# A layer kernel whose instruction order is planned again: transfers served one after another, loads set later, three-pass first tiles, warm-up in gaps

## The chip, the cores and the metric

The kernel runs on one core of a Trainium2 chip. The metric is device time in microseconds (us), the median of several executions; lower is better. The core has a matrix engine (TensorE, PE in the profile), a vector engine (VectorE, DVE), an activation engine (ScalarE, ACT), GpSimd (POOL) and a queue engine (SyncE, SP) that issues most transfers. Each engine works through its own list of instructions in order: an instruction that waits holds back all that stand behind it on that engine.

## The reference

The input x is 2048 tokens of 512 values. With xn, the layer-normed x, the output is x plus an attention part plus a part from a mixture of experts:

```
xn  = layernorm(x)
qkv = xn @ wqkv                       # 512 x 1536, 32 heads of 16
out = x + attention(qkv) @ wo         # each token sees itself and 7 tokens
                                      # at distances 2, 4, .. 14 before it
    + sum over the token's two best experts e of
        gate_e * (silu(xn @ w1[e]) @ w2[e])   # 8 experts, 512 -> 1792 -> 512
```

The two experts of a token are the largest of xn @ w_gate, and the gates are the softmax of those two logits.

## The kernel before

**Numbers.** Every float32 operand of a product is split into a high and a low float16 part (scales SW, SX, SH), and each product is three matmuls: high by high, low by high, high by low. In the QKV products these are the passes h, l and w.

**Stages on TensorE.** First the QKV products: 64 tile products, column group cg (0 to 3) by token tile j (0 to 15), named q<cg>_<j>; group 0 carries the router's logits too. A tile product is 12 matmuls (lines 348 and 350), about 2 us. They go through six PSUM banks, and ScalarE copies each result out (line 358, `ev`) into one of three buffers `qe`, from which four tiles at a time are stored to DRAM (line 367, `qst`). Then eight experts, 14 blocks each: `up` (lines 779 to 781), SiLU on ScalarE (line 787, tile hs), the split into hh (lines 793 and 797) and `down` (lines 809 to 822). At the end the product with wo (line 905).

**The token tiles' way to TensorE.** For each tile j, VectorE takes mean and variance (lines 279, 281), ScalarE the root (line 286), VectorE the normalized tile xn (lines 291, 293); `hi` (ScalarE, line 298) and `lo` (VectorE, line 302) make the float16 parts xh. TensorE needs them with the token in the free dimension (xnT): the first six tiles are turned on TensorE (line 313), the other ten by a transposing transfer `tn` of xh (line 308), issued by SP. All 16 tiles xh are also stored to DRAM (line 305, `xst`), from where the rows of each expert are gathered later. xh has six buffers: `hi` of tile j waits for both transfers of tile j-6. The QKV weights come in four groups of 768 KB (line 250, `lwq0` to `lwq3`) and are split by ScalarE and VectorE (lines 265, 262).

**The way to the experts.** After the last logits (line 363) VectorE works out the lists of rows (lines 391 to 503). GpSimd gathers the rows of an expert in up to five pieces (line 708, tile xg, five buffers), and SP issues a transposing transfer for each piece (line 715, tile xgt, `tx<e>_<t>`). Expert weights come in 57 pieces `ld<U>` of 1 MB (lines 730, 735, tile s, two buffers); ScalarE and VectorE split each (lines 745 and 754, `whi`, `wlo`). Beside this, VectorE does the attention: line 635, 639 (scores), ScalarE's exponential (line 649, `ax`), lines 662, 668 and so on, most of them 4.4 us long.

**What sets the order.** Class Plan holds every step as a task: engine, duration, dependencies, priority, and `land`, the time from a transfer's issue to its arrival. `solve` gives each task a latest time, going back from TensorE's order, and then goes forward in time: each engine takes, of the tasks that are ready, the one with the earliest latest time. `emit` writes the instructions in the order found. On the chip nothing of the planned times is left, only the order on each engine and the waits for data and buffers. The memory of xnT, the weights of QKV and `qe` is given to the expert stage by `swap_left`; the planner lets the first SiLU follow once the last `qst` has been issued, but on the chip hs takes memory that this transfer has to be done reading.

Of the kernel before, what the change touches and what calls it, by code (L numbers as in the profile page):

```python
# [44 lines left out]
WARM = 14  # L45
N32 = 6
NPE = 6
NPAIR = 8
XB = 8
NG = E * FB  # L50
# [3 lines left out]
class Plan:  # L54
    SAME = {"PE": 0.0, "DVE": 0.0, "ACT": 0.0, "SP": 0.0, "POOL": 0.0}

# [3 lines left out]
    def add(self, name, eng, dur, fn, deps=(), prio=0.0, land=0.0, early=0.0, begun=()):  # L60
        assert name not in self.tasks, name
        self.tasks[name] = (eng, dur, fn, [d for d in deps if d is not None], prio, land, early,
                            [d for d in begun if d is not None])

    def solve(self, start):
# [9 lines left out]
        for n in sorted((n for n in tk if tk[n][0] == "PE" and tk[n][4] > -900), key=lambda n: tk[n][4]):  # L75
            due[n] = at
            at += tk[n][1]
        late, todo, wait = {}, [n for n in tk if n not in outs], {n: len(o) for n, o in outs.items()}
        while todo:
            n = todo.pop()  # L80
            t = tk[n]
            l_ = due.get(n, at)
            for o in outs.get(n, ()):
                l_ = min(l_, late[o] if n in tk[o][7] and n not in tk[o][3] else late[o] - t[1] - t[5] - 0.08)
# [8 lines left out]
        begin, end, order = {}, {}, []  # L93

        def release(n):
# [11 lines left out]
        while True:  # L107
            best = None
            for e, lst in ready.items():
# [3 lines left out]
                c = min((p, r, n) for r, p, n in lst if r <= t0)  # L113
                if best is None or (t0, c[0]) < best[0]:
                    best = ((t0, c[0]), e, c)
# [6 lines left out]
            end[n] = t0 + t[1] + t[5]  # L122
# [6 lines left out]
        self.begin, self.end, self.order = begin, end, order  # L129
# [19 lines left out]
def layer_kernel(ctx: ExitStack, tc, x, wqkv, wo, wg, w1, w2, out):  # L149
# [38 lines left out]
    def c_first():  # L188
        v.memset(warm, 0.0)
        v.memset(eps, 1e-5 / (SX * SX))  # L190
# [37 lines left out]

    def warm_up(n):
        t = py.tile([P, D], F32, name="pwarm", tag="y0")  # L230
        for _ in range(n):
            nc.tensor.matmul(t, warm[:, 0:P], warm, start=True, stop=True)
# [3 lines left out]
    def load_x(g, h=None):  # L236
# [3 lines left out]
        nc.sync.dma_start(X[g][:, c_], xv[:, 2 * g:2 * g + 2, :][:, c_])  # L240
# [43 lines left out]
    def ln_rs(j):  # L284
        rs = fre.tile([P, 1], F32, name=f"rs_{j}", tag="rs", bufs=4)
        nc.scalar.activation(rs, L[j]["mv"][:, 1:2], AF.Sqrt, bias=eps, scale=1.0 / (SX * SX))
        L[j]["rs"] = rs

    def ln_nm(j):
        rs = L[j]["rs"]  # L290
        v.reciprocal(rs, rs)
# [989 lines left out]
```

## Time and profile before

| what | value |
|---|---|
| median of 3 runs | 807.27 us (805.89 to 807.44) |
| the profiled execution's own time | 804.93 us |
| its span, first to last instruction | 803.2 us |
| TensorE busy | 771.4 us, 96% of the span |
| VectorE busy | 624.8 us, 78% |
| ScalarE busy | 356.1 us, 44% |
| GpSimd busy | 115.3 us, 14% |
| mean granted TensorE clock | 0.990 of full speed |

The profile is one execution. In it, "busy" is time with an instruction running on the engine; a bracket behind a row of the timeline is the engine's idle time just before, and what ended it. SPq and ACTq rows are the issuing of transfers by SP and ACT. "PEclk" is the granted TensorE clock as a share of full speed, and the DMA share is the mean busy share of the 16 DMA engines (it can go over 1).

### The profile page before, as it was taken

To read this page: it belongs to the slowest core of one execution; us is meant where nothing else is said; L and a number is where in the kernel's file an instruction comes from. 1 tells how busy PE (TensorE), PEld (TensorE's weight loads), DVE (VectorE), ACT (ScalarE), POOL (GpSimd) and SP (SyncE) were. 2 spreads that over 40 slices of the span, in tenths; PEclk is the share of its full clock that TensorE was granted. 3 is DMA by queue.
4 is the path that set the end of the run, shared out by engine and by line. 5 is a ranking of instruction groups with operands and counts; after the bars stand their busy time and mean duration, and the time that the engine had idled before them with its cause. 6 is when DMAs were issued, how large, how long until landed. Compare 5 with 4: busy or idle time off the path is not lost.

```text
span 803.2 us, 13105 instructions
## 1 busy us (share of the span) xinstructions
PE 771.4 (96%) x5300; PEld 426.4 (53%) x5300; DVE 624.8 (78%) x591; ACT 356.1 (44%) x523; POOL 115.3 (14%) x103
## 2 busy tenths in 40 slices
PE   7978998969999999999999999999999999999996
PEld 3634665535556555555555555555555555555543
DVE  5861985999999999999999999999994333366074
ACT  4542331444445544745464465455464544544100
POOL 2000072400016001300100050010000000063061
PEclk8999999989999999999999999999999999999999
DMA  8599699943548656834894585477439833455184
GB/s 288 149 274 238 218 238 294 340 150 106 180 104 268 211 145 172 277 105 145 234 258 154 182 196 170 153 157 259 136 105 264 302 110 108 140 189 168 50 275 147
DMA packets 147075, 153.88 MB, mean 192 GB/s; under 512 B 67729, under 2 KB 115217, under 8 KB 146499
## 3 DMA queue, kind: packets, MB, share of 16 engines
q1 hardware_dynamic: 139667, 135.33, 56.2%
q0 software_dynamic: 5216, 16.88, 6.9%
q10 hardware_dynamic: 2128, 0.80, 0.4%
q8 instruction: 43, 0.70, 0.4%
q14 instruction: 21, 0.17, 0.1%
HBM read 108.12 MB, written 29.56 MB: 171 GB/s over the span
## 4 chain that ended last, share of the span: by engine, by line
PE 87%; DMA 6%; DVE 3%; ACT 1%; SPq 1%; issue 1%; ACTq 0%; POOL 0%; DVEq 0%
PE pu L779 12%; PE pu L780 12%; PE pu L781 12%; PE y L811 9%; PE y L809 9%; PE y L810 9%; PE pq L350 6%; PE pw L905 5%; PE yt L820 3%; PE yt L822 3%; PE yt L821 3%; PE pq L348 3%; DMA xnT<-xh 2%; DMA s<-in_B_w 1%; DVE at L639 1%; DMA xg<-xr,lis 1%
## 5 line engine op out<-in xcount | busy, mean ns | idle before, releaser
L779 PE MATMUL pu<-xgt,w 128*128 128x64 f16 (+8 forms) x616 | 185.2, 322 | 7.4 <-ACT hs L787 7.4
L780 PE MATMUL pu<-xgt,w 128*128 128x64 f16 (+8 forms) x616 | 185.3, 322 | 0.0
L781 PE MATMUL pu<-xgt,w 128*128 128x64 f16 (+8 forms) x616 | 181.0, 322 | 0.0
L787 ACT ACTIVATE hs<-pu 128x64 f32<-128x64 f32 (+8 forms) x154 | 69.5, 480 | 201.2 <-PE pu L781 200.4
L754 DVE SCALAR_TENSOR_TENSOR w<-s,w 128x2048 f16<-128x2048 f32 (+1 forms) x57 | 128.1, 2249 | 34.6 <-ACT w L745 34.2
L745 ACT ACTIVATE w<-s 128x2048 f16<-128x2048 f32 (+1 forms) x57 | 107.2, 1882 | 74.3 <-PE yt L822 62.1
L708 POOL DMA_INDIRECT xg<-xr,lis x35 | 72.5, 2071 | 465.1 <-DMA xgt<-xg 352.9
L811 PE MATMUL y<-w,hh 128*128 128x512 f16 x336 | 127.3, 379 | 0.0
L810 PE MATMUL y<-w,hh 128*128 128x512 f16 x336 | 127.3, 379 | 0.0
L809 PE MATMUL y<-w,hh 128*128 128x512 f16 x336 | 127.3, 379 | 0.0
L797 DVE SCALAR_TENSOR_TENSOR hh<-hs,hh 128x550 f16<-128x550 f32 (+7 forms) x112 | 76.6, 686 | 48.5 <-ACT hh L793 48.5
L350 PE MATMUL pq<-wq,xnT 128*128 128x384 f16 (+1 forms) x512 | 96.1, 331 | 15.1 <-DMA xnT<-xh 8.0
L781 PEld LDWEIGHTS <-w 128*128 128x128 f16 x616 | 59.2, 98 | 48.9 <-issue 0.8
L780 PEld LDWEIGHTS <-w 128*128 128x128 f16 x616 | 59.3, 98 | 48.7 <-issue 8.2
L779 PEld LDWEIGHTS <-w 128*128 128x128 f16 x616 | 59.6, 98 | 41.1 <-issue 0.5
L821 PE MATMUL yt<-hh,w 128*128 128x166 f16 (+7 forms) x448 | 81.0, 219 | 0.0
L820 PE MATMUL yt<-hh,w 128*128 128x166 f16 (+7 forms) x448 | 80.9, 219 | 0.0
L822 PE MATMUL yt<-hh,w 128*128 128x166 f16 (+7 forms) x448 | 80.9, 219 | 0.0
L635 DVE TENSOR_TENSOR pq<-kt,qt 128x4096 f32<-128x4096 f32 x16 | 70.7, 4421 | 7.7 <-DMA qt<-qd 7.5
L350 PEld LDWEIGHTS <-xnT 128*128 128x128 f16 x512 | 49.6, 98 | 50.6 <-DMA xnT<-xh 12.1
L793 ACT ACTIVATE hh<-hs 128x550 f16<-128x550 f32 (+7 forms) x112 | 70.6, 630 | 3.5
L662 DVE TENSOR_TENSOR pv<-vt,at 128x4096 f32<-128x4096 f32 x16 | 70.8, 4423 | 0.3
(165 smaller groups left out, 861.7 us busy)
## 6 DMA issues: line engine op xcount, KB each, us to landing
s<-in_B_w SPq DMA_DIRECT2D x112, 512.0 KB
qd<-qe SPq DMA_DIRECT2D x16, 768.0 KB
kt<-qd SPq DMA_DIRECT2D x8, 960.0 KB
vt<-qd SPq DMA_DIRECT2D x8, 960.0 KB
yd<-ys SPq DMA_DIRECT2D x24, 256.0 KB
xr<-xh SPq DMA_DIRECT2D x16, 256.0 KB
qt<-qd SPq DMA_DIRECT2D x8, 512.0 KB
acc<-in_A_x SPq DMA_DIRECT2D x4, 1024.0 KB
```

Of the source, the lines that this page charges most:

```text
L350: nc.tensor.matmul(ps[:, 0:n], xs, t[:, kb, 0:n], start=st, stop=False)
L745: nc.scalar.activation(w[:, 0, c_], stg[k][:, c_], AF.Copy, scale=SW)
L754: v.scalar_tensor_tensor(w[:, 1, c_], stg[k][:, c_], SW, w[:, 0, c_], op0=ALU.mult, op1=ALU.subtract)
L779: nc.tensor.matmul(ps, a_[:, 0, kb, fs], xh, start=kb == 0, stop=False)
L780: nc.tensor.matmul(ps, a_[:, 0, kb, fs], xl, start=False, stop=False)
L781: nc.tensor.matmul(ps, a_[:, 1, kb, fs], xh, start=False, stop=kb == KB - 1)
L809: nc.tensor.matmul(y_, hi, b_[:, 0, :], start=st, stop=False)
L810: nc.tensor.matmul(y_, hi, b_[:, 1, :], start=False, stop=False)
L811: nc.tensor.matmul(y_, lo, b_[:, 0, :], start=False, stop=sp)
L820: nc.tensor.matmul(y_, b_[:, 0, cs], hi, start=st and c % 2 == 0, stop=False, skip_group_check=True)
L821: nc.tensor.matmul(y_, b_[:, 0, cs], lo, start=False, stop=False, skip_group_check=True)
L822: nc.tensor.matmul(y_, b_[:, 1, cs], hi, start=False, stop=sp, skip_group_check=True)
```

## The change

The arithmetic stays the same in kind: the scale SX moves from the normalization into the instructions that make the float16 parts, so a copy becomes an activation with a scale, and a subtraction becomes a multiply and subtract. The order is planned with other rules, and some transfers change engine. The diff, cut to its core:

```diff
 # Plan: `land` becomes `svc`, the time a transfer occupies the one server;
 # `lead`: not ready earlier than so long before its latest time
-            end[n] = t0 + t[1] + t[5]
+            end[n] = t0 + t[1]
+            if t[5]:
+                dma = max(dma, t0 + 1.3) + t[5]
+                end[n] = dma + 0.7
...
+            if t[5]:
+                r += min(max(0.0, late[n] - r) / 4, 3.0)
+            if t[8] is not None:
+                r = max(r, late[n] - t[8])
...
+    add("root", "ACT", 1.6, lambda: nc.scalar.activation(root, eps, AF.Sqrt if not POW else AF.Copy), early=0.3)
+    for i in range(NFILL):                                    # NFILL = 6
+        add(f"warm{i}", "PE", mm(512), B(warm_up, 1), early=6.6, prio=1e6, begun=["T32_0"])
+    add("lx0", "SP", 0.45, B(load_x, 0, 0), svc=0.7, early=0.8)
-        add(f"lwq0_{kb}", "ACT", 0.62, B(load_wq, 0, [kb], nc.scalar), prio=-100 + kb, land=3.4 + 0.3 * kb, early=0.4)
-    add("lgate", "ACT", 0.62, B(load_gate, nc.scalar), prio=-90, land=3.0, deps=[], begun=["lwq0_3"])
-    add("root", "ACT", 1.5, lambda: nc.scalar.activation(root, eps, AF.Sqrt), begun=["lgate"], prio=-89)
-    add("lx1", "SP", 0.45, B(load_x, 0, 1), prio=1, land=3.0, begun=["lx0"])
+        add(f"lwq0_{kb}", "SP", 0.66, B(load_wq, 0, [kb], nc.sync), svc=0.67, begun=["lx0"])
+    add("lx1", "ACT", 0.6, B(load_x, 0, 1, nc.scalar), svc=0.7, begun=["root"])
+    add("lgate", "ACT", 0.6, B(load_gate, nc.scalar), svc=0.3, begun=["lx1"])
...
-    add("fills", "SP", 1.8, fills, deps=["lo_9"], prio=200, land=3.0)
+    add("fills", "SP", 1.2, fills, deps=["lwq1_3"], svc=1.2, early=20.0)
...
-        add(f"hi_{j}", "ACT", act(512), B(x_hi, j), deps=[f"nm_{j}", f"xst_{j - 6}" if j > 5 else None, ...
+        add(f"hi_{j}", "ACT", act(512), B(x_hi, j), early=18.0 if j < N32 else 0.0, deps=[f"nm_{j}", f"xst_{j - XH}" if j >= XH else None, ...
...                                                            # XH = 10 buffers of xh, 6 before
-            add(f"tn_{j}", "SP", 0.5, B(x_turn, j), deps=[f"lo_{j}"], prio=100 + j, land=5.5)
+            add(f"tn_{j}", "SP", 1.35, B(x_turn, j), deps=[f"lo_{j}"], svc=1.6)
...
-        if i < 4:
+        if i < NSPL:                                          # NSPL = 6
...
-                deps=["r_lis"] + prev + xst, prio=e, land=2.5)
+                deps=["r_lis"] + prev + xst, svc=0.9, lead=40.0 if e else None)
-                prio=G(e * FB - 8) if e else 20.0, land=5.5)
+                svc=1.6, lead=30.0 if e else None)
-        add(f"ld{U}", "SP", 1.4, B(piece_load, U), deps=[...], prio=G(2 * U - 6), land=6.5, ...
+        add(f"ld{U}", "SP", 1.0, B(piece_load, U), deps=[...], svc=3.0, lead=22.0, ...
```

All other transfers get an `svc` for their `land` too. The first six tile products (four before) are three tasks, h, l and w, that may stand apart, and the w passes may stand behind other tiles' passes. Six warm-up matmuls of 512 columns, on nothing but zeros, are set after the first transpose, beside the 14 at the start; they write a bank of their own. Functions that turned float16 tiles on TensorE go; no tile used them.

What this does to the order shows at three places. The first is SP's list in the QKV stage, about where the first token tiles have been normalized. xr<-xh is a store of a tile of xh, xnT<-xh a transposing transfer (the tile's number stands behind xh), wqs_2 and wqs_3 are the weights of the third and fourth column group, qd<-qe a store of results. Before:

```order
L305 DMA xr_67<-xh_2_273 128x1024
L367 DMA qd_66<-qe_0_0_236 128x6x256
L367 DMA qd_66<-qe_1_0_280 128x6x256
L250 DMA wqs_2_500<-in_A_wqkv 128x3x128 x4
L305 DMA xr_67<-xh_3_328 128x1024
L308 DMA_TRANSPOSE xnT_102<-xh_7_480 128x8x128
L305 DMA xr_67<-xh_4_331 128x1024
L305 DMA xr_67<-xh_7_480 128x1024
L250 DMA wqs_3_556<-in_A_wqkv 128x3x128 x4
L305 DMA xr_67<-xh_5_401 128x1024
L308 DMA_TRANSPOSE xnT_102<-xh_8_530 128x8x128
```

After:

```order
L253 DMA x_7_252<-in_A_x 128x1024
L263 DMA wqs_2_270<-in_A_wqkv 128x3x128 x4
L263 DMA wqs_3_320<-in_A_wqkv 128x3x128 x4
L378 DMA qd_66<-zf_85 8x16x64 x2
L379 DMA xr_67<-zf_85 512x1x128
L325 DMA_TRANSPOSE xnT_102<-xh_6_403 128x8x128
L374 DMA qd_66<-qe_0_0_247 128x6x256
L322 DMA xr_67<-xh_6_403 128x1024
L322 DMA xr_67<-xh_0_318 128x1024
L325 DMA_TRANSPOSE xnT_102<-xh_7_499 128x8x128
L374 DMA qd_66<-qe_1_0_307 128x6x256
```

The weights of the later groups and the fills now stand right behind the loads of x, ahead of the first transposing transfer; they stood between the second and third. The stores of the first tiles stand behind, among the transposing transfers.

The second place is SP's list toward the end of the QKV stage. xgt_1<-xg_1 are the transposing transfers of the second expert's five pieces, s<-in_B_w1 and in_B_w2 the halves of a piece of expert weights, kt and qt attention loads; rows named ISA, which move no data, are left out. Before:

```order
L715 DMA_TRANSPOSE xgt_1_1355<-xg_1_1_1329 128x8x128
L730 DMA s_3_1381<-in_B_w1 128x4x256
L735 DMA s_3_1381<-in_B_w2 128x2x512
L715 DMA_TRANSPOSE xgt_1_1355<-xg_1_2_1333 128x8x128
L715 DMA_TRANSPOSE xgt_1_1355<-xg_1_3_1353 128x8x128
L715 DMA_TRANSPOSE xgt_1_1355<-xg_1_4_1376 128x8x32
L367 DMA qd_66<-qe_2_3_1349 128x6x256
L367 DMA qd_66<-qe_3_0_1431 128x6x256
```

After:

```order
L374 DMA qd_66<-qe_2_3_1339 128x6x256
L737 DMA s_2_1557<-in_B_w1 128x4x256
L742 DMA s_2_1557<-in_B_w2 128x2x512
L374 DMA qd_66<-qe_3_0_1436 128x6x256
L737 DMA s_3_1608<-in_B_w1 128x4x256
L742 DMA s_3_1608<-in_B_w2 128x2x512
L374 DMA qd_66<-qe_3_1_1555 128x6x256
L374 DMA qd_66<-qe_3_2_1624 128x6x256
L737 DMA s_4_1705<-in_B_w1 128x4x256
L742 DMA s_4_1705<-in_B_w2 128x2x512
L374 DMA qd_66<-qe_3_3_1687 128x6x256
```

The second expert's transposing transfers stood ahead of the stores qe_2_3 and qe_3_0; now none of them stands ahead of the last store qe_3_3 (they come after the next pair of attention loads and s_5), and pieces of weights stand between the stores.

The third place is ScalarE's list at the end of the QKV stage: copies out of PSUM into qe_3_3 (the last four tiles), the attention's second exponential at_1, and the first SiLU, hs_0_0. Before:

```order
L358 ACTIVATE qe_3_3_1638<-pq_3_12_1607 128x3x2x64
L649 ACTIVATE at_1_1452<-at_1_1452 128x512
L358 ACTIVATE qe_3_3_1638<-pq_3_13_1625 128x3x2x64
L358 ACTIVATE qe_3_3_1638<-pq_3_14_1644 128x3x2x64
L358 ACTIVATE qe_3_3_1638<-pq_3_15_1660 128x3x2x64
L787 ACT_TABLE_LOAD
L787 ACTIVATE hs_0_0_1744<-pu_0_0_0_1675 128x486
```

After:

```order
L365 ACTIVATE qe_3_3_1687<-pq_3_12_1659 128x3x2x64
L365 ACTIVATE qe_3_3_1687<-pq_3_13_1673 128x3x2x64
L365 ACTIVATE qe_3_3_1687<-pq_3_14_1691 128x3x2x64
L365 ACTIVATE qe_3_3_1687<-pq_3_15_1708 128x3x2x64
L794 ACT_TABLE_LOAD
L794 ACTIVATE hs_0_0_1793<-pu_0_0_0_1723 128x486
```

The exponential, which stood ahead of the last three copies, now stands behind the third SiLU.

On VectorE, the small steps that work out the gates (lines 510 to 592 of the kernel before; they ran from 590 to 605 us there, with other work between) move to the time right after the first attention scores, ahead of the first split of expert weights.

More of the change, by code (lines that the diff above doesn't have):

```diff
@@ L54, with add @@
 class Plan:
-    SAME = {"PE": 0.0, "DVE": 0.0, "ACT": 0.0, "SP": 0.0, "POOL": 0.0}
     def __init__(self):
         self.tasks = {}
-    def add(self, name, eng, dur, fn, deps=(), prio=0.0, land=0.0, early=0.0, begun=()):
+    def add(self, name, eng, dur, fn, deps=(), prio=0.0, svc=0.0, early=0.0, begun=(), lead=None):
         assert name not in self.tasks, name
-        self.tasks[name] = (eng, dur, fn, [d for d in deps if d is not None], prio, land, early,
-                            [d for d in begun if d is not None])
+        self.tasks[name] = (eng, dur, fn, [d for d in deps if d is not None], prio, svc, early,
+                            [d for d in begun if d is not None], lead)
     def solve(self, start):
@@ L82, in solve @@
             l_ = due.get(n, at)
+            cost = t[1] + 0.08 + (2.5 + t[5] * 1.5 if t[5] else 0.0)
             for o in outs.get(n, ()):
-                l_ = min(l_, late[o] if n in tk[o][7] and n not in tk[o][3] else late[o] - t[1] - t[5] - 0.08)
+                l_ = min(l_, late[o] if n in tk[o][7] and n not in tk[o][3] else late[o] - cost)
             late[n] = l_
@@ L226, in layer_kernel, with load_x @@
     xrv = xr[0:S, :].rearrange("(p j) d -> p j d", j=NJ)
+    pwarm = py.tile([P, D], F32, name="pwarm", tag="yt1")
     def warm_up(n):
-        t = py.tile([P, D], F32, name="pwarm", tag="y0")
         for _ in range(n):
-            nc.tensor.matmul(t, warm[:, 0:P], warm, start=True, stop=True)
+            nc.tensor.matmul(pwarm, warm[:, 0:P], warm, start=True, stop=True)
     X = {}
-    def load_x(g, h=None):
+    def load_x(g, h=None, eng=nc.sync):
         if g not in X:
@@ L318, in x_ev32 @@
         if lo:
-            v.scalar_tensor_tensor(xnT[:, KB + ks.start:KB + ks.stop, j * P:(j + 1) * P], L[j]["pt"][:, ks], 1.0, hi,
+            v.scalar_tensor_tensor(xnT[:, KB + ks.start:KB + ks.stop, j * P:(j + 1) * P], L[j]["pt"][:, ks], SX, hi,
                                    op0=ALU.mult, op1=ALU.subtract)
         else:
-            nc.scalar.copy(hi, L[j]["pt"][:, ks])
-    def x_pe16(j):
-        pt = py.tile([P, 2 * KB, P], F16, name=f"pt_{j}", tag="misc" if j % 2 else "yt0")
-        for a in range(2 * KB):
-            nc.tensor.transpose(pt[:, a, :], L[j]["xh"][:, a // KB, (a % KB) * P:(a % KB + 1) * P], ident)
-        L[j]["pt"] = pt
-    def x_ev16(j, lo):
-        ks = slice(KB * lo, KB * lo + KB)
-        (v.tensor_copy if lo else nc.scalar.copy)(xnT[:, ks, j * P:(j + 1) * P], L[j]["pt"][:, ks])
+            nc.scalar.activation(hi, L[j]["pt"][:, ks], AF.Copy, scale=SX)
     qtags = [(pu, "up"), (pu, "up"), (py, "y0"), (py, "y1"), (py, "y2"), (py, "yt1")]
```

108 lines of the change are left out of this document (57 added, 51 removed).

## The prediction

> **What bounds the kernel now.** I read the page's busy times first:
>
> ```profile
> PE 771.4 (96%) x5300; PEld 426.4 (53%) x5300; DVE 624.8 (78%) x591; ACT 356.1 (44%) x523; POOL 115.3 (14%) x103
> ```
>
> TensorE (PE) is busy for 771.4 of 803.2 us, so at most 31.8 us of waiting can go, and time in which it ran at a low clock. The stages tell where they lie (columns: window, its length, busy us of PE, PEld, DVE, ACT, POOL with counts, granted clock, DMA share, GB/s):
>
> ```profile
> 0.00:10.00 10.00, 6.22 (x18) 2.31 (x18) 3.28 (x10) 2.54 (x6) 5.69 (x36) 0.98 0.83 244
> 10.00:20.00 10.00, 7.96 (x36) 4.38 (x37) 8.46 (x23) 5.97 (x17) 0.00 (x0) 0.68 0.91 335
> 20.00:30.00 10.00, 10.00 (x67) 6.59 (x65) 8.49 (x23) 6.92 (x17) 0.00 (x0) 1.00 0.15 55
> 40.00:50.00 10.00, 8.45 (x51) 4.62 (x48) 7.75 (x22) 5.46 (x13) 0.00 (x0) 1.00 1.30 299
> 50.00:60.00 10.00, 6.36 (x36) 3.36 (x36) 5.00 (x15) 2.90 (x8) 0.00 (x0) 1.00 0.91 251
> 60.00:70.00 10.00, 5.84 (x33) 3.08 (x34) 1.22 (x4) 1.56 (x4) 0.00 (x0) 1.00 1.13 258
> 170.00:180.00 10.00, 10.00 (x77) 5.29 (x75) 9.48 (x7) 6.20 (x11) 0.00 (x0) 0.83 0.26 85
> 180.00:300.00 120.00, 120.00 (x969) 70.24 (x967) 115.83 (x70) 60.18 (x89) 15.22 (x5) 1.00 0.56 170
> 780.00:803.20 23.20, 17.08 (x103) 8.93 (x101) 10.38 (x17) 0.00 (x0) 3.12 (x3) 0.96 0.50 167
> ```
>
> From 180 us on TensorE has no gap until the last 6.1 us, which are the last results' way out and stay. So everything to be won lies ahead of 180 us, at four places: the start, 40 to 70 us (9.35 us idle), and two that TensorE's waits name:
>
> ```profile
> PE pq L350 <- DMA xnT<-xh: 8.0, 4, 2.6
> PE pu L779 <- ACT hs L787: 7.4, 1, 7.4
> PE pq L350 <- ACT qe L358: 3.0, 2, 2.8
> ```
>
> (us in total, times, the longest). As from 180 us on TensorE alone sets the pace, what it reaches earlier there is earlier at the end, as long as nobody else falls behind.
>
> **a, the start.** TensorE's and then ScalarE's timeline:
>
> ```profile
> 1.27 5.59 PE L232 MATMUL pwarm<-warm 128*128 128x512 f16 x14 [1.27 <-DVE eps L190]
> 11.61 1.49 PE L350 MATMUL pq<-wq,xnT 128*128 128x400 f16 x4 [2.66 <-ACT rs L286]
> 20.70 0.60 PE L313 MATMUL pt<-ident,xn 128*128 128x128 f32 x4
> 40.20 1.52 PE L350 MATMUL pq<-wq,xnT 128*128 128x400 f16 x8
> 42.21 1.46 PE L350 MATMUL pq<-wq,xnT 128*128 128x384 f16 x8
> 5.72 1.28 ACT L931 ACT_TABLE_LOAD   x1 [5.72 <-DMA wqs<-in_A_wqkv]
> 9.55 1.35 ACT L265 ACTIVATE wq<-wqs 128x384 f16<-128x384 f32 x3 [1.73 <-DMA wqs<-in_A_wqkv]
> ```
>
> The first product starts at 11.61, 2.06 us after the last of the first group's weights has landed (9.55): two more steps on ScalarE. Until then the transfers were loaded (share 0.83, 244 GB/s with the empty start), with 0.77 MB of these weights, half a MB of the first two tiles of x, and as much again of later weights and tiles issued between. After, what is needed first is also queued first: 1.31 MB at 244 GB/s, the mean with the empty start in it, are 5.4 us from the first issue at 0.8 on: 6.2. With the 2.06 behind it, and some of the landing's own delay, the first product starts between 8.3 and 9; the router's small weights, which now follow the second tile of x on ScalarE's queue, could hold it until 10. I take 8.8. Then come three tile products, each 2.01 us (from 40.20 to 42.21), or 6.0 where the clock is full, and what ran from 20.70 to 40.20 (19.5 us without a gap, the same work), with one filler: the product that started at 40.20 (group 0, tile 6) starts at 34.5. Against it stand small waits for VectorE, which was 85% busy from 20 to 30 (8.49 of 10); I take 35.2, a gain of **5.0**, bounds 2 and 6. Part of this is the clock: in the window from 10 us on it was 0.68, worth at most 0.32 x 7.96 = 2.5 us. With the tiles split into passes, and the w passes later, TensorE waits for the second half of the weights less; the fillers (six of at most 0.4 us, 5.59 / 14) lie in gaps.
>
> Now a rule against this edit. The trace has an issue of such a transfer by SP at 0.70 us, and four of them now stand ahead of all later loads:
>
> ```profile
> 1.75 0.70 SPq L250 DMA_DIRECT2D wqs<-in_A_wqkv  x1
> ```
>
> The Trainium skill (Trainium Kernel Development and Optimization, Key Constraints) says that all queues share the same 16 DMA engines, and that issuing from several engines saves the issue time alone. By that, taking four issues from ScalarE to SP gives back up to 4 x 0.70 = 2.8 us, and the gain of a would be 2.2. I do not take it, as the share of 0.83 says that the transfers themselves, not their issuing, were the limit; it lies within the bounds.
>
> **b, 40 to 70 us.** TensorE waits for transposing transfers. In the chain of waits one takes
>
> ```profile
> 46.40 5.52 DMA xnT<-xh
> ```
>
> from issue to landing, and the DMA share in 4 us stretches (columns as above) says why they come late:
>
> ```profile
> 28.00:32.00 4.00, 4.00 (x28) 2.56 (x27) 3.65 (x10) 2.69 (x6) 0.00 (x0) 1.00 0.08 16
> 64.00:68.00 4.00, 1.78 (x11) 1.09 (x12) 0.17 (x1) 0.22 (x1) 0.00 (x0) 1.00 1.17 223
> 44.40 0.62 ACT L298 CAST xh<-xn 128x512 f16<-128x512 f32 x1 [1.50 <-DMA xr<-xh]
> 30.36 1.36 SPq L308 DMA_TRANSPOSE xnT<-xh  x1
> ```
>
> There is a hole with nothing to transfer, and then a jam, in which 1.5 MB of later weights and the fills go ahead of transposing transfers, and `hi` waits for stores to free xh. The change moves these weights into the time before the hole and gives xh ten buffers. Their eight issues, 0.70 us each, and the fills' pass 8 us of SP's list, behind the loads of x; the first transposing transfer was issued at 30.36, and after, nothing for it can be ready before VectorE has gone through seven tiles, so SP has the time. What is late next is VectorE, whose work for all 16 tiles is, by the groups
>
> ```profile
> L279 DVE BATCH_NORM_STATS2 bs<-x 128x6 f32<-128x512 f32 x16 | 11.0, 686 | 3.3 <-DMA x<-in_A_x 3.3
> L302 DVE TENSOR_TENSOR xh<-xn,xh 128x512 f16<-128x512 f32 x16 | 10.7, 679 | 3.8 <-ACT xh L298 3.8
> L293 DVE TENSOR_SCALAR xn<-x,mv,rs 128x512 f32<-128x512 f32 x16 | 8.7, 546 | 0.6
> ```
>
> 30.4 us, and some 13 with the aggregation, the reciprocals, the weights' splits and the results of the transposes. It starts at about 4, and if it waits 3 us on the way it has the last tile by 51; 5.5 us later, at 56 or 57, that tile is turned. TensorE asks for it twelve products of 2.01 us after 35.2, at 59. So the wait goes, with 2 to 3 us to spare, and if the transfers need that much more, some of it stays. I take the 9.35 us, 1.4 more for the restarts behind each gap, and 1.5 off: **9.3**, bounds 4 and 10.8. The other instructions (a copy becomes an activation, a subtraction a multiply and subtract of the same shape) I cost at nothing.
>
> **c, 3.0 us at 138.** SP's rows, and ScalarE's behind them:
>
> ```profile
> 129.66 4.28 SPq L715 DMA_TRANSPOSE xgt<-xg  x1
> 144.87 1.13 SPq L367 DMA_DIRECT2D qd<-qe  x2
> 138.65 1.91 ACT L745 ACTIVATE w<-s 128x2048 f16<-128x2048 f32 x1 [10.41 <-DMA s<-in_B_w]
> 158.70 0.63 ACT L649 ACTIVATE at<-at 128x512 f32<-128x512 f32 x1 [5.23 <-DVE at L646]
> 167.77 1.28 ACT L787 ACT_TABLE_LOAD   x1 [7.30 <-DMA qd<-qe]
> 169.06 0.69 ACT L787 ACTIVATE hs<-pu 128x486 f32<-128x486 f32 x2
> ```
>
> SP stood in the second expert's transposing transfers, which waited for gathered rows. The third piece of weights was behind them, so ScalarE stood 10.41 us in its split with the copies out of PSUM behind it, and TensorE found no bank. With those transfers later, the piece is issued when its buffer is free, far ahead of its split: **3.0**, bounds 0 and 3.0. What now stands in SP's list ahead of stores are weights that wait for VectorE; if VectorE is 6 us late, c stays gone and d suffers.
>
> **d, 7.4 us at 162.** Four more rows, of ScalarE, the chain, TensorE, and the windows (here window, length, PE busy, granted clock, DMA share, GB/s):
>
> ```profile
> 149.14 1.64 ACT L358 ACTIVATE qe<-pq 128x384 f32<-128x384 f32 x4 [4.36 <-DMA qd<-qe]
> 160.50 7.18 DMA qd<-qe
> 156.95 0.37 PE L779 MATMUL pu<-xgt,w 128*128 128x486 f16 x1
> 141.00:143.00 2.00, 2.00 (x12) 1.00 1.06 377
> ```
>
> The first SiLU waited for the last store of results, landed at 167.77, issued at 160.5: late because ScalarE's last copies stood behind the exponential (5.23 us). The restart ran at a mean granted clock of 0.83 from 170 to 180, so 1.7 us were lost. After, the copy follows the product by 0.5 us, the store lands 4.3 (the first of the pair issued at 144.87, by ScalarE's end of waiting at 149.14) to 7.3 us later, and table load and SiLU take 1.28 + 0.69 = 1.97. So TensorE goes on 6.8 to 9.8 us after its last QKV product; its first two blocks cover 5.5 (156.95 to 162.4, where the wait of 7.4 begins that the SiLU of 169.06 ends). A gap of 1.3 to 4.3 stays; I take 2.6, for the transfers are no longer jammed there, and no loss of clock: 7.4 + 1.7 - 2.6 = **6.5**, bounds 2 and 7.8. The wait of 2.8 us in c cost no clock (1.00 from 141 on), that of 7.4 did; what 4.3 would do no row shows, and with the 1.7 the lower bound is 2 or 3. The Trainium skill (TensorE: Matmul & The Clock Gate, What's actually happening) puts the drop at an idle window of about 3.4 us that runs freely. By that rule a gap of 4.3 would lose up to 1.7 us more and one of 2.6 nothing.
>
> **The sum.** 5.0 + 9.3 + 3.0 + 6.5 = 23.8 us, of the profiled execution's 804.93: 781.1. The median of the runs shown is 2.3 higher, 807.27, and less 23.8 it is 783.5. I predict 783. The small gate steps moved ahead on VectorE (some 10 us) are covered: TensorE then still has QKV products to do. Ten transposing pieces and the weights set later cost nothing as long as they land before ScalarE wants them; from 180 us on the transfers are 56% busy.
>
> **Rivals.** (1) The transfers stay the limit in b: 64 to 68 us shows a share of 1.17 with the PE waiting, and all the same bytes must pass. Then b is worth what the moved weights took, 1.5 MB at 335 GB/s or 4.5 us, a is lost, as TensorE only waits longer, and c and d are as above: gain 14, 793. For it speaks that stores of tiles are still between the transposing transfers; against it the empty stretch at 28. (2) VectorE comes late to the split of the third piece, since the gate steps are ahead of it; SP stands in the fifth piece, the last store behind it: d is lost, gain 17.3, 790. (3) Slower than before: the weights set later land too late for ScalarE's split, again and again; the SiLU stands behind it and TensorE runs dry. Of the 57 pieces of weights some 55 come while TensorE works on the experts; each would have to cost 23.8 / 55 = 0.43 us to bring the time back to 807. They are issued as soon as VectorE frees one of two buffers, if SP is not standing in something else; SP's new list has attention loads and transposes in between. Against it, before, ScalarE waited for a piece just once. At 0.6 us each, 816.
>
> **Chances.** My forecast 0.64, (1) 0.17, (2) 0.11, (3) 0.04, all else 0.04. The range goes from 777, all terms at their upper bounds (27.6 us off 804.93), to 794, which takes in (1) and (2). A change of 0.2% is about what a measurement of this kernel can tell. Faster 0.94, same 0.02, slower 0.04.
>
> **What would show it.** In the profile after: the first product at about 8.8 us and the clock not down at 10 to 17; no wait for xnT over 1 us between 35 and 60; the last QKV product done at 138 to 141; one gap of 1.3 to 4.3 us some 5.5 us later; no gap from there to the tail. Wrong would be idle TensorE beyond 180 us, or the tile products slowed by xnT.

## The result, and the profile after

The changed kernel takes 780.28 us (median of 4 runs, 780.26 to 782.59), beside 807.36 us (805.89 to 807.98) of the kernel before on the same chip: a ratio of 0.9674, 95% interval 0.9652 to 0.9696. The forecast of 783.0 lies 2.7 us above it. The profiled execution took 780.26 us, with a span of 778.3 us: 24.9 us shorter than the span before, where the forecast's sum was 23.8.

The page's line of TensorE, the windows that the prediction read before (window, length, busy us of PE, PEld, DVE, ACT, POOL with counts, granted clock, DMA share, GB/s), and all of TensorE's waits:

```profile
PE 766.5 (98%) x5306; PEld 426.0 (55%) x5306; DVE 625.8 (80%) x591; ACT 357.2 (46%) x523; POOL 104.4 (13%) x103
```

```profile
10.00:20.00 10.00, 10.00 (x63) 6.03 (x61) 8.86 (x23) 5.86 (x14) 0.00 (x0) 1.00 1.05 391
40.00:50.00 10.00, 10.00 (x62) 5.88 (x61) 8.54 (x23) 4.83 (x12) 0.00 (x0) 1.00 1.01 270
50.00:60.00 10.00, 10.00 (x63) 5.87 (x60) 1.78 (x8) 2.48 (x5) 0.00 (x0) 1.00 1.11 279
60.00:70.00 10.00, 10.00 (x63) 6.00 (x62) 6.44 (x24) 4.21 (x7) 0.00 (x0) 1.00 0.75 260
140.00:150.00 10.00, 8.16 (x72) 4.38 (x70) 7.88 (x8) 5.45 (x8) 0.00 (x0) 1.00 0.68 229
160.00:755.00 595.00, 595.00 (x4209) 325.67 (x4208) 482.75 (x329) 283.91 (x382) 78.30 (x53) 1.00 0.61 181
```

```profile
PE pt L330 <- DVE rs L308: 2.4, 1, 2.4
PE pu L786 <- ACT hs L794: 1.8, 1, 1.8
PE pwarm L245 <- DVE eps L202: 1.3, 1, 1.3
```

The waits for xnT and for ScalarE's copies have left the list. TensorE is busy through 40 to 70 us and from 160 to 755 us without a gap; one wait is left between the start and the tail, 1.8 us at the first SiLU.

Four rows of TensorE date the places: the first product, the product of group 0, tile 6 (40.20 us before), the end of group 0 (the 384-column product that starts there), and the first block of the experts (156.95 before):

```profile
10.54 2.70 PE L357 MATMUL pq<-wq,xnT 128*128 128x400 f16 x15
36.44 1.52 PE L357 MATMUL pq<-wq,xnT 128*128 128x400 f16 x8
62.33 1.46 PE L357 MATMUL pq<-wq,xnT 128*128 128x384 f16 x8
139.24 0.37 PE L786 MATMUL pu<-xgt,w 128*128 128x486 f16 x1
```

The third had this row in the kernel before:

```profile
76.68 1.46 PE L350 MATMUL pq<-wq,xnT 128*128 128x384 f16 x8
```

So the gain is 3.76 us at tile 6, 14.35 at the end of group 0, 17.71 at the first block, and 24.9 at the end of the span. By stages (the start up to tile 6, on to the end of group 0, on to the experts' first block, on to the end of the span): a 3.8, b 10.6, c 3.4, d 7.2.

The chain of waits at the first SiLU, and ScalarE and TensorE behind it:

```profile
139.96 4.44 DMA qd<-qe
144.48 1.28 ACT L794 ACT_TABLE_LOAD   x1 [4.55 <-DMA qd<-qe]
145.78 0.69 ACT L794 ACTIVATE hs<-pu 128x486 f32<-128x486 f32 x2
146.52 0.19 PE L786 MATMUL pu<-xgt,w 128*128 128x64 f16 x1 [1.84 <-ACT hs L794]
```

The last store is now issued half a us after the last QKV product's end, lands 4.44 us later, and table load and SiLU follow. The gap of 1.84 us cost no clock: the window from 140 us on is at 1.00.

### The profile page after: what moved, and what is told of

The parts are those of the page before. It is cut to its first block, busy times and chain, and to the rows that moved or that the text cites. A ratio compares the mean times of both kernels' runs of the same rounds, so it can differ in the third digit from the quotient of the medians.

```text
span 778.3 us, 13101 instructions
## 1 busy us (share of the span) xinstructions
PE 766.5 (98%) x5306; PEld 426.0 (55%) x5306; DVE 625.8 (80%) x591; ACT 357.2 (46%) x523; POOL 104.4 (13%) x103
## 4 chain that ended last, share of the span: by engine, by line
PE 97%; DMA 1%; DVE 0%; ACT 0%; issue 0%; SPq 0%; ACTq 0%
PE pu L786 12%; PE pu L788 12%; PE pu L787 12%; PE pq L357 11%; PE y L818 9%; PE y L817 9%; PE y L816 9%; PE pq L355 5%; PE pw L912 5%; PE yt L827 3%; PE yt L828 3%; PE yt L829 3%; PE yr L851 1%; DMA qd<-qe 1%; DMA wqs<-in_A_wqkv 1%; PE pt L330 0%
## 5 line engine op out<-in xcount | busy, mean ns | idle before, releaser
L715 POOL DMA_INDIRECT xg<-xr,lis x35 | 63.4, 1811 | 478.7 <-DMA xgt<-xg 391.4
L357 PE MATMUL pq<-wq,xnT 128*128 128x384 f16 (+1 forms) x512 | 94.2, 328 | 0.1
L646 DVE TENSOR_REDUCE at<-pq 128x256 f32<-128x4096 f32 x16 | 70.6, 4414 | 0.1
```

Source lines behind the costliest of these rows:

```text
L357: nc.tensor.matmul(ps[:, 0:n], xs, t[:, kb, 0:n], start=st, stop=False)
```

## The experiments

Theory: the four terms, each by its own cause. The main rivals are that the transfers' bulk or VectorE, and not the order, set b, c and d. Each kernel is compared with the kernel before on the same chip; the changed kernel's ratio is 0.9674 (0.9652 to 0.9696), so differences under some 2 us between two changed kernels are within the intervals, and there the profiles, one execution each, are what is left to go by.

**b done alone on the kernel before.** The transfers of the later QKV weights and the fills go ahead of the first store of a tile:

```diff
+    move(["lwq2", "lwq3", "fills"], "xst_0")     # ahead of it in the written order
```

> The kernel before with one thing moved: the weights of the third and fourth column group and the fills go in SP's list ahead of the first store of xh. Theory (the jam: these 1.6 MB stand ahead of the transposing transfers): TensorE's idle time from 40 to 70 us falls from 9.35 to about 5 us, time 802 to 803. Rival (the six buffers of xh alone hold the tiles back, the weights only fill time that is free): idle time there stays at 8 to 9.5 us, time 806 to 807.

Measured: 799.06 us, ratio 0.9885 (0.9843 to 0.9927). TensorE's waits for xnT, 8.0 us in the kernel before, and the two windows that still have a gap:

```profile
PE pq L350 <- DMA xnT<-xh: 2.7, 1, 2.7
```

```profile
50.00:60.00 10.00, 7.68 (x45) 4.13 (x43) 6.06 (x18) 4.03 (x10) 0.00 (x0) 1.00 1.11 305
60.00:70.00 10.00, 9.65 (x57) 5.51 (x58) 0.52 (x3) 1.96 (x4) 0.00 (x0) 1.00 1.00 247
```

The same bytes pass with a DMA share as high as before, and 6.7 of the 9.35 us of idle time from 40 to 70 us are gone (2.32 + 0.35 are left). That is more than was expected of this edit alone, in part because this execution came to tile 6 1.2 us later (41.42 against 40.20), which leaves the transfers as much more time. From tile 6 to the end of group 0 TensorE took 29.1 us, where the kernel before took 36.5 and the changed kernel 25.9: some 7.4 of the 10.6 us of b. It was the place of these transfers in the order, not the amount of bytes, that made TensorE wait.

**b undone in the changed kernel.** The same transfers go back to about where they stood before, between stores and transposing transfers. (In the kernel before, the weights of the third group were issued between the first and the second transposing transfer, at 34.05, those of the fourth between the second and the third, at 43.08, and the fills between the fourth and the fifth, at 51.76; the description of the change puts all of them between the second and the third.)

```diff
+    move(["lwq2"], "xst_1")
+    move(["lwq3", "fills"], "tn_9")
```

> The changed kernel with the weights of the third and fourth column group and the fills put back into SP's list among the transposing transfers (third group behind the second store of results, fourth group and fills ahead of the transposing transfer of tile 9). Theory (the jam): TensorE waits for xnT again, 3 to 5 us between 35 and 60 us, time 783.5 to 785. Rival (ten buffers of xh are enough): no such wait over 1 us, time 780 to 781.

Measured: 787.11 us, ratio 0.9724 (0.9688 to 0.9761), more than the theory had.

```profile
PE pq L357 <- DMA xnT<-xh: 5.1, 4, 2.8
```

Four waits are back, 5.1 us where the kernel before had 8.0. From tile 6 to the end of group 0 TensorE took 31.7 us, 5.8 more than in the changed kernel. The profiled execution lost 7.9 us of span, more than that: it had also started with a lower clock, which the experiment with the fillers takes up.

**The ten buffers of xh.** Planned anew with the six of before:

```diff
-XH = 10
+XH = 6
```

> The changed kernel with six buffers instead of ten for the high halves of the rows of x that wait for their trip through memory, planned anew. Theory (what took the waits for transposed rows out of 40 to 70 us is that the weights' pieces go behind the stores and transposes; six buffers are then nearly enough): ScalarE waits for a store of a row block once or twice, the tensor engine waits up to 2 us more in 40 to 70 us, and the time is 780 to 782.5. Rival (the ten buffers carry the gain): waits for transposed rows of 4 to 9 us in that stage as before, and the time 784 to 789.

Measured: 781.99 us, ratio 0.969 (0.966 to 0.9721). TensorE is busy without a gap:

```profile
50.00:60.00 10.00, 10.00 (x62) 5.87 (x60) 1.74 (x8) 2.86 (x6) 0.00 (x0) 1.00 1.07 300
```

ScalarE does not wait for a store of a tile at all, not even the once or twice that the theory allowed. The buffers carry nothing of b as long as the weights are out of the way. Whether they are what kept the other half of b when the weights went back was not tried. The 1 us in the profile (span 779.3) lies at the first SiLU, where the other plan left a gap of 2.8 us.

**c and d done alone on the kernel before.** The second expert's transposing transfers, and the third's gathers, behind the sixth piece of weights:

```diff
+    move(tx1 + ga2, o[o.index("ld5") + 1])     # all tx1_*, ga2_*
```

> The kernel before with one thing moved: the second expert's five transposing transfers go in SP's list behind the sixth piece of weights, as in the change. Theory (SP stood in them, and weights, attention loads and stores behind it): the wait of 3.0 us for a PSUM bank goes, the 7.5 us in which VectorE waited for the attention's second load go, so the exponential no longer holds ScalarE's copies and the gap at the first SiLU shrinks from 7.4 to 2 to 4 us; time 797 to 799. Rival (it is the exponential's place in ScalarE's list that costs, whatever SP does): the 3.0 us go, the 7.4 us stay within 1 us, time 803.5 to 805.

Measured: 802.01 us, ratio 0.9916 (0.9886 to 0.9945), between the two. ScalarE's waits in order of time, then TensorE's:

```profile
138.05 1.91 ACT L745 ACTIVATE w<-s 128x2048 f16<-128x2048 f32 x1 [8.46 <-DMA s<-in_B_w]
158.11 0.63 ACT L649 ACTIVATE at<-at 128x512 f32<-128x512 f32 x1 [6.87 <-DVE at L646]
163.67 1.28 ACT L787 ACT_TABLE_LOAD   x1 [3.79 <-DMA qd<-qe]
```

```profile
PE pu L779 <- ACT hs L787: 3.9, 1, 3.9
PE pq L350 <- ACT qe L358: 1.1, 2, 0.9
```

With the transposes out of SP's way (and the third expert's gathers, which the expectation does not name), about half of c and d is gained. The other half stands on ScalarE: the exponential still stands ahead of the last three copies, waits 6.87 us for VectorE, and the last store is late by as much.

**The exponential put back in the changed kernel,** with the steps that lead to it, and a weight split and a weight load ahead of them; the transposes are left late:

```diff
+    k = [n for n in ("wlo2", "ld4", "qk1_1", "qs1_1", "am1", "ax1") if o.index(n) > o.index("ev(3, 13)")]
+    move(k, "ev(3, 13)")     # ax1: the exponential
```

> The changed kernel with one piece of its order put back: the loads and products of the first weighting's scores and its exponential stand ahead of the last three copies of the queries' product on ScalarE, as in the kernel before; the transposes of the gathered rows stay late. Theory (the 7.4 us at the first SiLU of before came from copies that stood behind the exponential's wait, so that the last store and all that follows it came late): the copies wait for the exponential, the store is issued 4 to 7 us later, the gap at the first SiLU is back at 5 to 9 us instead of 1.84, the clock falls after it, and the time is 784 to 790. Rival (the gap came from the transposes that SyncE stood in, which stay late here): the gap stays under 3 us and the time is 780 to 782.

Measured: 789.83 us, ratio 0.9778 (0.9754 to 0.9802). ScalarE, SP's issue of the last store, and TensorE's waits:

```profile
146.15 0.63 ACT L656 ACTIVATE at<-at 128x512 f32<-128x512 f32 x1 [11.95 <-DVE at L653]
146.69 1.23 ACT L365 ACTIVATE qe<-pq 128x384 f32<-128x384 f32 x3
147.95 0.37 SPq L374 DMA_DIRECT2D qd<-qe  x1
```

```profile
PE pu L786 <- ACT qe L365: 4.9, 1, 4.9
PE pu L786 <- ACT hs L794: 3.1, 1, 3.1
```

The three copies stood 11.95 us behind the exponential, the store was issued at 147.95 and not at 139.96, and TensorE lost 8.0 us in two waits, one for the banks and one for the SiLU. In the changed kernel this step alone costs as much as the whole of d. The wait is longer than the 5.23 us of the kernel before, so the run shows what such a place in the list can cost, not how much of d was due to it there.

**The transposes put back in the changed kernel,** with the gathers that feed them; the exponential is left late:

```diff
+    move([n for n in o if n.startswith("ga1_")], "ak1")
+    move(["tx1_0"], "aq1")
+    move(["tx1_1", "tx1_2", "tx1_3", "tx1_4"], "qst2_3")
```

> The changed kernel with the second expert's five transposing transfers put back in SP's list ahead of the store of the third column group's last tiles and of the third piece of weights. Theory: SP stands in them until about 122 us, ScalarE waits in the split of the third piece, TensorE waits 2 to 4 us for a PSUM bank, and the gap at the first SiLU grows from 1.8 by 1 to 4 us; time 784 to 788. Rival (with the gathers done in time the place in the list costs nothing): no wait for a bank, the gap within 1 us of 1.8, time 780 to 781.

Measured: 789.44 us, ratio 0.976 (0.9722 to 0.9798). ScalarE with SP's issue of the last store, and the window of its landing:

```profile
131.44 0.49 ACT L365 ACTIVATE qe<-pq 128x384 f32<-128x384 f32 x1 [7.04 <-DMA qd<-qe]
141.53 0.71 SPq L374 DMA_DIRECT2D qd<-qe  x1
151.13 1.28 ACT L794 ACT_TABLE_LOAD   x1 [10.69 <-DMA qd<-qe]
```

```profile
140.00:150.00 10.00, 4.78 (x34) 2.37 (x33) 9.86 (x5) 0.45 (x2) 0.00 (x0) 0.90 1.09 392
```

No wait for a bank comes back, so as an account of c this edit missed; but a gap of 8.38 us at the SiLU does. Its mechanism is another: the stores that were held up by the transposes all go out behind one another, at 392 GB/s, and the last one, issued from 141.53 on, is in at 151.13: 9.6 us, where 4.44 were needed. In the changed kernel either cause of d is enough for a gap of that size, and with the transposes alone out of the way in the kernel before 3.9 us were left: the change had to take both away. On the size of c, six executions show how long ScalarE stood and what TensorE then waited for banks: 10.41 us and 3.0 (before), 8.46 and 1.1 (the transposes late), 10.12 and 3.4 (the weights early), 12.23 and 3.4 (the load of x moved, below), 11.95 and 4.9 (the exponential early), and 7.04 and none here. In the five with a wait the six banks covered 6.7 to 8.8 us of the standing.

**The start's loads issued as before.** ScalarE again issues the first weights and the gate's, with the root behind them, SP both tiles of x; planned anew:

```diff
-        add(f"lwq0_{kb}", "SP", 0.66, B(load_wq, 0, [kb], nc.sync), svc=0.67, begun=["lx0"])
-    add("lx1", "ACT", 0.6, B(load_x, 0, 1, nc.scalar), svc=0.7, begun=["root"])
+        add(f"lwq0_{kb}", "ACT", 0.62, B(load_wq, 0, [kb], nc.scalar), svc=0.67, early=0.4)
+    add("lx1", "SP", 0.45, B(load_x, 0, 1), svc=0.7, begun=["lx0"])
...
```

> The changed kernel planned anew with the start's loads issued as in the kernel before: the first weight piece and the gate on ScalarE, the root behind them, both tiles of x on SyncE. Theory (the start gained because the root no longer stands behind ScalarE's issues, and because the first pieces land earlier): the first product of queries starts at 11.3 to 12 us instead of 10.54, the clock falls in the window from 10 to 20 us, and the time is 782 to 784, 2 to 4 above the changed kernel. Rival (the transfers set the start, who issues them changes only the issue time, and the three passes over the weight are what gained): first product within 0.4 us of 10.54, the time 780 to 781.

Measured: 784.39 us, ratio 0.9706 (0.9686 to 0.9726). The time is close to the 782 to 784 of the theory, but not for its reason. TensorE's first product, its first block of the experts, and ScalarE at the first SiLU:

```profile
10.90 2.36 PE L357 MATMUL pq<-wq,xnT 128*128 128x400 f16 x13
146.74 1.28 ACT L794 ACT_TABLE_LOAD   x1 [6.89 <-DMA qd<-qe]
```

```profile
139.16 0.37 PE L786 MATMUL pu<-xgt,w 128*128 128x486 f16 x1
```

The first product is 0.36 us later, the clock there full, and the experts begin at 139.16, 0.08 earlier than in the changed kernel: in a plan made anew, who issues the loads, and where the root stands, is worth nothing here. What was lost lies at the SiLU, where the last store landed 6.89 us after ScalarE had its copy done instead of 4.55. The gap is 4.2 us, and behind it the clock fell:

```profile
150.00:160.00 10.00, 10.00 (x72) 5.32 (x71) 9.96 (x8) 5.16 (x8) 0.00 (x0) 0.88 0.25 86
```

With 0.95 in the window before (5.82 us busy) that is about 1.5 us of clock, an estimate from the two windows. With the 2.4 us of longer gap it accounts for the 4.0 us of span. The store was issued at the same time (139.87 against 139.96); what other transfers held it up was not tried by itself. My theory of the start fell.

**The early load of x moved, in the kernel before.** Half a MB, the third and fourth tile of x, stood among the first weights; it goes behind them:

```diff
+    move(["lx2"], o[o.index(k[-1]) + 1])     # k: the four lwq1
```

> The kernel before with one load moved: the half MB of the third and fourth tile of x, which stood among the start's weight pieces, goes behind the last piece of the second group; the issuing engines, the root's place, the two passes of a product and the missing fillers stay. Theory (what gained at the start is the order of the transfers: what is needed first is queued first): the first product starts at 10.5 to 11 us instead of 11.61, the clock of the window from 10 to 20 us rises from 0.68 to 0.85 or more, and 2 to 3 of the start's 3.8 us come with this one line, some of which the later waits for transposed rows may take back: ratio 0.996 to 0.999 (1 to 3 us). Rival (the passes and the fillers carry it): first product within 0.3 us of 11.61, no change.

Measured: 807.08 us, ratio 0.9973 (0.9954 to 0.9992). The gain of some 2 us is of the size that the theory had, but the first product moved by 0.2 us only, as the rival had it.

```profile
11.41 1.34 PE L350 MATMUL pq<-wq,xnT 128*128 128x400 f16 x4 [3.00 <-DVE wq L270]
10.96 0.18 DVE L269 TENSOR_SCALAR wq<-gs 128x32 f16<-128x32 f32 x1 [2.84 <-DMA gs<-in_B_w_gate]
```

The first product waited 3.00 us for the router's weights, 16 KB, which stood behind the four pieces on ScalarE's queue. In the changed kernel they are issued at 1.71, and no one waits for them. Beside that the profile shows the clock at 0.83 in the window from 10 to 20 us (0.68 before), and at the first SiLU a gap of 5.5 us instead of 7.4, far from the edit. So the load of x alone was not what held the start, and where the 2 us come from stays open.

**The fillers left out** of the changed kernel (zeros against zeros, so the output does not depend on them):

```diff
-        add(f"warm{i}", "PE", mm(512), B(warm_up, 1), early=6.6, prio=1e6, begun=["T32_0"])
+        add(f"warm{i}", "PE", mm(512), B(warm_up, 0), early=6.6, prio=1e6, begun=["T32_0"])
```

> The changed kernel in the same order, with the six filling products of the start (zeros against zeros, 0.86 us in one row directly ahead of the first product of queries) left out; the output does not depend on them. Theory (the fillers lie in gaps but for the last four, which stand ahead of a product whose operand was nearly ready): the first product starts 0.4 to 0.9 us earlier, at 9.7 to 10.1, the granted clock of the window from 10 to 20 us stays at 1.00, and the time falls by about 0.5, to 779.5 to 780. Rival (the fillers keep the clock up across the start): the clock of that window falls to 0.7 to 0.9 and the time is 781 to 783.

Measured: 780.31 us, ratio 0.9652 (0.9632 to 0.9671). The first product, and the experts' first block:

```profile
10.17 3.05 PE L357 MATMUL pq<-wq,xnT 128*128 128x400 f16 x11
139.45 0.37 PE L786 MATMUL pu<-xgt,w 128*128 128x486 f16 x1
```

The first product came 0.37 us earlier; the clock fell all the same (0.72 from 7 to 13 us), and by 139 us the balance was 0.21 us against this kernel: no difference in the profiles. The four runs lie in two pairs, 779.7 and 780.9; the profiled one is of the upper pair, and no trace shows whether the lower pair kept the clock, as the theory has it for 779.5 to 780. Nor do the fillers hold the clock surely. Six of the profiled kernels (the changed one, and those with the weights late, the transposes early, the exponential early, six buffers, and the SiLU's own place) have the same order at the start, fillers in it. In four of them the first product came at 10.54 to 10.62 at full clock, in two at 11.97 and 12.02, with the clock down.

**The start's order on VectorE and ScalarE changed,** the first tile's steps ahead of the second tile's. Directly ahead of the first product the trace has five fillers, four in the changed kernel; the one that the expectation names did not come about:

```diff
+    move(["rs_0"], "wh0_0")
+    move(["nm_0"], "wl0_0")
+    move(["T32_0", "warm0", "warm1", "warm2", "warm3", "warm4", "eh_0_0", "eh_0_1"], "wh0_2")
...
```

> The changed kernel with the written order of the start changed, nothing else: on VectorE and ScalarE the first tile's normalization stands ahead of the second tile's statistics, its copies ahead of the last two weight pieces, and one filler instead of four directly ahead of the first product. Theory (the first product came at 10.54 and not at 8.8 because the first tile's last steps stood behind the second tile of x, which landed late, and behind the fillers): the first product at 8.4 to 9.2, the clock still 1.00, and the time 1.2 to 2 us lower, ratio 0.965 to 0.967 of the kernel before where the changed kernel has 0.9674. Rival (the weight's pieces, landing until about 8, and the splits behind them set it): the first product at 9.8 to 10.5, or waits inside the first three products that take the gain back; time within 0.6 us of the changed kernel's.

Measured: 780.44 us, ratio 0.9655 (0.9626 to 0.9684): the rival's outcome. TensorE's first rows, and its first block of the experts:

```profile
8.68 0.98 PE L357 MATMUL pq<-wq,xnT 128*128 128x400 f16 x4
10.30 0.66 PE L330 MATMUL pt<-ident,xn 128*128 128x128 f32 x4 [0.63 <-DVE xn L310]
10.79 2.43 PE L357 MATMUL pq<-wq,xnT 128*128 128x400 f16 x12
```

```profile
139.39 0.37 PE L786 MATMUL pu<-xgt,w 128*128 128x486 f16 x1
```

The first product starts at 8.68, just where the prediction wanted it, and nothing comes of it: behind its first four matmuls TensorE turns to the second tile and waits 0.63 us for its normalization, and the experts begin 0.15 us later than in the changed kernel. The time of the first product is no measure of this start. The five runs lie within 0.3 us, the four of the changed kernel within 2.3. TensorE idles less ahead of the first product here, and a start that always keeps its clock would look so, but that is not shown.

**A place of its own for the SiLU's results,** so that the first SiLU need not wait for the last store's landing:

```diff
+        hsp = pool("hsp", 3, reuse_waits="tile")
-        hs = hsd[key, f] = mop.tile([P, CT], F32, name=f"hs_{key}_{f}", tag="hs", bufs=3)
+        hs = hsd[key, f] = hsp.tile([P, CT], F32, name=f"hs_{key}_{f}", tag="hs", bufs=3)
```

> The changed kernel with the SiLU's results in a place of their own, which the queries' staging buffers do not share, so that the first SiLU waits for its product and no longer for the last store's landing. Theory (the 1.84 us that are left at that place are that landing alone): no gap over 0.4 us at the first SiLU, and the time 1.3 to 2 us lower, ratio to the kernel before 0.9645 to 0.966. Rival (the table load, 1.28 us, and VectorE, which is busy with the scores until 145, are next and nearly as late): a gap of 0.8 to 1.8 us stays, time the same within 0.8 us.

Measured: 779.11 us, ratio 0.9636 (0.9609 to 0.9663). ScalarE, and the window of TensorE:

```profile
141.42 1.28 ACT L795 ACT_TABLE_LOAD   x1
143.37 0.69 ACT L795 ACTIVATE hs<-pu 128x486 f32<-128x486 f32 x2 [0.67 <-PE pu L789]
```

```profile
140.00:150.00 10.00, 10.00 (x83) 5.39 (x81) 9.34 (x9) 6.47 (x10) 0.00 (x0) 1.00 0.70 242
```

The SiLU waits for its product and no more, and the gap is gone. The whole 1.84 us was the store's landing. This execution had the start with the low clock (first product at 12.02), and its span is still 0.7 us shorter than the changed kernel's.

**Both edits.**

> The changed kernel with both of the two edits before, the results' own place and the start's order. Theory (two places one behind the other on one engine's chain: their gains add): 2.5 to 4 us lower than the changed kernel, 776.5 to 778, ratio 0.962 to 0.9645 of the kernel before. Rival (what comes earlier at the start is waited for again in the rows' trip from 40 to 70 us, or at the SiLU): the better of the two alone, 778.5 to 779.5.

Measured: 778.54 us (5 runs, 777.96 to 778.76), ratio 0.963 (0.9601 to 0.9659), span 776.4: 1.9 us less than the changed kernel, which is the place alone. The rival was right, the start's order adds nothing to the best times. It is the best of the kernels here by its median; its interval overlaps that of the changed kernel.

## Why the prediction was right

Its sum was 23.8 us and the span gave 24.9. Three of the four terms lie inside their bounds; c, at 3.4, is above its upper bound of 3.0. That the sum is so close is in part luck: a was 1.2 us too high, and b, c and d together 2.3 too low. What the runs show to have caused b, c and d is among the causes named; for a it is not. Point by point:

**a, 5.0 forecast, 3.8 measured, the one term whose working failed.** The failing step is "the first product starts between 8.3 and 9 ... I take 8.8". It started at 10.54. Two rows of VectorE and ScalarE show what stood ahead: VectorE takes the second tile's statistics, at 6.89, ahead of the first tile's normalization, at 7.87, and the last two weight splits stand on ScalarE behind the second tile's root. The statistics come no sooner because VectorE stands in a weight split until then (the last section has its row):

```profile
6.89 0.68 DVE L292 BATCH_NORM_STATS2 bs<-x 128x6 f32<-128x512 f32 x1
8.03 0.92 ACT L278 ACTIVATE wq<-wqs 128x384 f16<-128x384 f32 x2
```

But the step's logic failed too, as the reordered start showed: with the first product at 8.68, what stood behind it waited. Four arrangements of the start, with first products from 8.68 to 10.90, all bring the experts to 139.16 to 139.45. What the start gained is at most 2.5 us of clock (0.68 before in the window from 10 us on, full after; the prediction's bound) and the rest, 1.3 us or more, in products that come earlier. The clock's part is not sure of every execution: in two of six it fell, and the one whose row can be compared lost 1.5 us by the experts' first block. How much of a the passes carry was not tried apart.

Against the rule weighed there (Trainium Kernel Development and Optimization, Key Constraints, in the Trainium skill: issuing from several engines saves only the issue time), the prediction held that the transfers themselves were the limit. The experiment does not contradict the rule, which speaks of issue time alone: with the issues back on ScalarE the experts began 0.08 us earlier, so that time was not what TensorE waited for here. The 2.8 us that I worked out from it as a charge did not come, nor did any gain from it. Whether the transfers themselves were the limit this does not show.

**b, 9.3 forecast, 10.6 measured.** The 1.5 us taken off for a remainder were not needed; no wait is left. VectorE, forecast to be done with the last tile by 51, makes its low part at 51.60, to 52.29. Undoing the weights' place brings 5.1 us of waits back, doing it alone takes 6.7 away. What the rest of b owes to the stores of tiles, now behind the transposes, was not tried apart. Of the two means named, the weights and the ten buffers, the first carries the gain, and with it done the second adds nothing. Rival (1), the transfers as the limit, is refuted: the same bytes at a share of 1.01 and 1.11, no wait.

**c, 3.0 forecast, 3.4 measured, and d, 6.5 forecast, 7.2 measured.** c is 0.4 us more than the 3.0 of waits because the forecast added no restarts there, as it did in b; this is the likely reason, not a shown one. The cause of c is shown from one side: with the transposes late in the kernel before 1.1 of the 3.0 us were left, but putting them back brought no wait for a bank. The gap left at the SiLU is 1.84 (1.3 to 4.3 expected, 2.6 taken), the landing 4.44 (4.3 to 7.3). For d the prediction named the exponential, and the jam of transfers only in passing ("no longer jammed there"). The runs show each as enough by itself in the changed kernel, and the transposes' place as half of c and d in the kernel before. Rival (2), VectorE late for the third piece, did not come: the last store was issued half a us after the last QKV product, and ScalarE waited for weights at most 2.1 us at a time, 10.4 before. Rival (3), weights landing too late again and again, did not either: not a gap from 160 to 755 us.

## What to carry to other kernels

Where a gap has two causes that stand one behind the other on different engines, taking one away may gain only half (3.9 of 7.4 us were left here), and putting either one back may cost all: read the chain back past the first cause before costing an edit. Forecast a start by the time at which the matrix engine has its work without a gap, not by its first product. A transfer that nobody waits for still belongs in the sum if it stands ahead, in its queue or in the shared engines, of one that somebody waits for.

## What the runs showed of the hardware

**An idle time of 2.4 us sometimes costs the clock.** The changed kernel idled 2.40 us ahead of its first transposes and kept the clock at 1.00; the kernel with the SiLU's own place idled 2.37 us in the same order, and its windows read (window, length, PE busy, clock, DMA share, GB/s):

```profile
8.00:9.00 1.00, 0.45 (x2) 0.59 1.19 287
9.00:10.00 1.00, 1.00 (x5) 0.50 1.00 308
```

The clock was back by 12 us, and the experts began 1.47 us later (140.71 against 139.24). The Trainium skill (TensorE: Matmul & The Clock Gate, Why this matters for your kernels) advises against gaps over some 3 us. At the start, gaps of 1.95 us (the weights late), 2.13 (no fillers) and 2.37, with little work behind them, took the clock down here, while one of 2.40 did not. In the middle of full work, at the first SiLU, the rows agree with the advice: gaps of 1.84 and 2.8 us (six buffers) left the clock at 1.00, and gaps of 3.9 (the transposes late), 4.2 (the loads as before) and 8.4 (the transposes early) took it to 0.83, 0.88 and 0.58 over 10 us. So a gap of 4.3 us, for which the prediction had no row, would most likely have cost clock too.

**A VectorE instruction beside a GpSimd instruction that had begun ended only behind it.** In the kernel with the reordered start the first tile's normalization, 0.55 us elsewhere, ran while GpSimd made the attention mask; in the changed kernel, with the mask at 5.03 for 1.70 us, a weight split did, also 0.55 us elsewhere (its row is the last):

```profile
5.24 1.75 DVE L310 TENSOR_SCALAR xn<-x,mv,rs 128x512 f32<-128x512 f32 x1
5.02 1.70 POOL L225 TENSOR_SCALAR_AFFINE_SELECT mask<-mask 128x512 f32<-128x512 f32 x1
6.02 0.95 DVE L275 SCALAR_TENSOR_TENSOR wq<-wqs,wq 128x384 f16<-128x384 f32 x1 [1.13 <-ACT wq L278]
```

The normalization took 1.75 us and ended 0.27 us behind GpSimd's instruction (6.99 and 6.72). With both edits it started at 5.49 and ended at 6.99 too, and the split ended at 6.97: the end does not depend on the start. The Trainium skill (SBUF — State Buffer, SBUF: two separate sides) has VectorE and GpSimd share a pair of ports, which whichever starts first holds for its whole instruction while the other blocks; for VectorE it names instructions in a mode that uses two ports, or with two inputs in SBUF beside a GpSimd instruction that reads it. The rows agree in that VectorE ends last; that 0.27 us behind GpSimd's end were enough for an instruction of 0.55 us they leave open. The mask could be made at another time; whether that helps the start was not tried.
